# One more seven-product gate pair in chunk 1, batch 4's casts behind the masks, and a sum of u moved in chunk 3

## The chip, the core and the metric

The kernel runs on one core of one Trainium2 chip. The metric is the device time of a whole execution in microseconds (us), as the median of several runs. TensorE (PE) does the matrix products, VectorE (DVE), ScalarE (ACT) and GpSimd (POOL) the elementwise work, and the queues of SyncE (SP), POOL and ACT issue the transfers. Everything is float16 on chip, with float32 sums.

## The reference

Attention over 8 batches and 8 heads (576 positions, 64 wide), then a gated feed-forward block over all 4608 tokens:

```python
mask_plain = (rel >= 0) & (rel < 32)
mask_dil = (rel >= 0) & (rel < 128) & (rel % 4 == 0)
# heads 0..3 take mask_plain, heads 4..7 take mask_dil
attn = softmax(where(mask, q @ k.T / 8, -1e9))
x = (attn @ v).transpose(0, 2, 1, 3).reshape(4608, 512)
g = x @ w_gate                          # 512 -> 1536
val = x @ w_val                         # 512 -> 1536
out = (gelu(g) * val) @ w_out           # 1536 -> 512
```

## The kernel before

The tokens are cut into 9 chunks of 512. A chunk `c` has two stages. In its gate stage the two products with `w_gate` and `w_val` are made for 12 column blocks `nb` of 128, ACT takes the gelu of the one (`g`, L1032), and DVE multiplies it with the other into `u_all` (`u`, L1037). In its output stage `u_all` is multiplied with `w_out`, and between these products stands the attention of later tokens: four pairs of heads `n`, four to a batch, so that pairs 16 to 19 are batch 4. For a pair there are scores `S`, their exponential `P` (ACT, L488), the product with the 0/1 mask `M` (DVE, L493), denominators `D`, numerators `N`, logarithm and reciprocal `l`, `r` (ACT), and the product `X` into `xT` (DVE, L618). In output stage 2 the pairs 12 to 15 are worked on, and at its end stand the scores of pairs 16 and 17.

From chunk 1 on the output product of a pair of blocks uses seven half-size products for eight (`seven`, L816). It needs sums of `u` on DVE (`u_sums`, word `k j@part@n`: part 0 is L777, part 1 L782, part 2 L784; part 2 is read by the last product alone) and sums of `w_out`, made once (`weight_sums`, word `K i@part`, L764 to L770). The gate products of some block pairs `j` (blocks 2j and 2j+1) are done the same way in chunks 2 to 8 (`IN_PLACES`): word `f j@product@bank` is four matmuls of 256 columns (L696), whose results ACT keeps (L710, L718) or DVE adds (`quarter`, L720), with a gelu and a product by halves (L728, L737). That needs four sums of x (`x_sums`, word `x`, L678: DVE in chunks 1 and 2, POOL in chunks 3 to 7) and four sums of the gate weights, once (`gate_sums`, word `h`, L661). Pair 1's are made in output stage 0 already.

The order on every engine is written by hand: `gate_words(c)` and `out_words(c)` give a list of words; a number takes so many matmuls off the chunk's list, and each other word emits the instructions of one step. `BLOCKS[c]` gives, for the directly computed blocks, how many `f` steps follow each half block and which words stand there. Each engine works its own instructions in that order, and waits on semaphores for the others.

A batch comes in by float32 loads into three areas of `stage`, casts on POOL into `s16` (`cast_plain`, L217, two for q and two for k; `cast_dil`, L229), and four DMA transposes from `s16` into the q/k buffer (`turn`, L272): plain q, plain k, dilated q, dilated k, in this order. The load of dilated k goes into the area that plain q was in, and so waits for plain q's casts. All these loads, the transposes, the loads of v and the stores of results are issued by SP in program order, with one queue. Word `R`, at the start of gate stage 2, emits the rest of batch 3 and all of batch 4.

TensorE is kept busy from the start by 69 matmuls of 32x32 and four of 512 columns on a constant (`warm`, L909) before the first data come.

Of the kernel before, what the change touches and what calls it, by code (L numbers as in the profile page):

```python
# [14 lines left out]
SYNC = mybir.DependencyInfo(mybir.DependencyClass.Sync, mybir.DependencyReason.DATA)  # L15
# [6 lines left out]
def kernel(  # L22
# [10 lines left out]
    nc = tc.nc  # L33
    B, H, S, D = q.shape
# [177 lines left out]
            rest = src[b, x * HK : x * HK + HK, S - 64 : S, :].rearrange("h p d -> p h d")  # L212
            nc.sync.dma_start(out=st[64 * x : 64 * x + 64, 4], in_=rest)

    def cast_plain(t, i):
        for g in range(2):
            nc.gpsimd.tensor_copy(  # L217
                s16[:, 1280 * t + 640 * g : 1280 * t + 640 * g + 640].rearrange("p (k c) -> p k c", k=5),
                st_of(i).rearrange("p (k g c) -> p k g c", k=5, g=2)[:, :, g],
            )  # L220

    def load_dil(src, b, i):
        rows_ = src[b, HK:H, 0 : 4 * P, :].rearrange("h (p r) d -> p h (r d)", r=4)
# [48 lines left out]
        nc.sync.dma_start_transpose(out=dst, in_=src)  # L272
# [695 lines left out]
    def gate_banks(c, nb):  # L968

        if c == 0:  # L970
            return ((4, 5), (6, 7))[nb] if nb < 2 else ((0, 1), (2, 3))[nb % 2]
        if c in IN_SEVEN:
            if c == NCH - 1:
                return (3, 5) if nb == 10 else (0, 7)
            if c == NCH - 2:
                return (2, 5) if nb == 10 else (0, 7)
            if nb in (1, 11):
                return (1, 4)
            return (4, 1) if nb == 9 and c < 4 else (0, 7)
        return ((0, 7), (1, 6) if c == 1 else (1, 4))[nb % 2]  # L980

    SEVEN = range(1, NCH)

# [29 lines left out]
    def run_program(c, words, mms, banks):  # L1013

        units = {"S": two_s, "M": two_m, "D": two_den, "N": two_num, "T": two_t, "B": two_b, "X": two_x, "A": two_a, "l": two_l, "r": two_r, "P": two_p_of, "t": turn_first, "y": turn_second, "c": cast_six, "W": idle, "b": bias_first}
        joint = {"S": two_s_mms, "D": two_den_mms, "N": two_num_mms}
        for word in words.split():
            kind, args = word[0], [] if "+" in word else [int(x) for x in word[1:].split("@") if x]
            if "+" in word:
                lists = []  # L1020
                for part in word.split("+"):
                    n, at = (int(x) for x in part[1:].split("@"))
                    lists.append((joint[part[0]](n, at), odd(n)))
                emit_tiles(*lists)
            elif kind.isdigit():
                for _ in range(int(word)):
                    mms.pop(0)()
            elif kind in units:
                units[kind](*args)
            elif kind == "g":  # L1030
                g = ffn.tile([P, CH], F16, tag="g")
                nc.scalar.activation(g, ps[:, gate_banks(c, args[0])[0], :], AF.Gelu)  # L1032
                tiles["g", args[0]] = g
            elif kind == "u":
                nb = args[0]
                val = ps[:, gate_banks(c, nb)[1], :]
                nc.vector.scalar_tensor_tensor(u_all[:, nb, :], tiles.pop(("g", nb)), -USCALE if c in SEVEN and nb % 2 else USCALE, val, ALU.mult, ALU.mult)  # L1037
            elif kind in "ew":
                at = args[1] if len(args) > 1 else c
                store(at, args[0], out_banks(at)[args[0]], "act" if kind == "e" else "dve")  # L1040
            elif kind == "k":
                u_sums(*args)
            elif kind == "K":
                weight_sums(*args)
            elif kind == "f":
                j, product, place = args
                ffn1_seven(c, j, product, place, product in (1, 2, 7))
                quarter_u()
                quarter_gelu()
                quarter_out(c, j, product, place)  # L1050
            elif kind == "U":
                quarter_u()
                quarter_gelu()
            elif kind == "h":
                gate_sums(*args)
            elif kind == "x":
                x_sums(args[0] if args else c)
            elif kind == "q":
                what, eng, at = (args + [c])[:3]
                part_out(at, what, eng, out_banks(at)[what in (1, 3, 5)])  # L1060
            elif kind == "L":
                mms.clear()
                last_chunk(c)
            elif kind == "V":
                (second, second_v)[args[0] if args else 0]()
            elif kind == "v":
                cast_part(c + 2, args[0], tiles["M"])
            elif kind == "z":
                cast_part(c + 1, args[0])
            elif kind == "F":  # L1070
                load_first(args[0])
            elif kind == "H":
                load_rest(args[0])
            elif kind == "R":
                load_rest(3)
                load_first(4)
                load_rest(4)
            elif kind == "E":
                nc.scalar.preload_act_table_set("natural_log_exp_and_others")
            else:  # L1080
                nc.scalar.preload_act_table_set("gelu_and_others")
        assert not mms

    def gate_words(c):
# [13 lines left out]
        if c == min(SEVEN):  # L1098
            for n, nb in enumerate((1, 2, 2, 4, 4, 4, 5, 6, 6, 8, 8, 8)):
                sums[nb] += f" K{n // 4}@{n % 4}"  # L1100
        before = "" if c == NCH - 1 else f"q6@1@{c - 1}"
        last = f" u{NNB - 1} k5@0 k5@1 k5@2" if c > 6 else ""
        first = "7 G 1 g0 2 u0 4 g1 2 u1" if c < NCH - 1 else ""
        if c in IN_SEVEN:
            words = seven_words(c)
            loads = f"{loads} x" if c == 2 else f"x z0 z1 {loads}" if c == 3 else f"x z1 {loads}" if c < 6 else "x z1 h3@0 h3@1 h3@2 h3@3" if c < 7 else "x" if c < NCH - 1 else loads
# [4 lines left out]
        if c == 1:  # L1111
            blocks[8] += f" S{2 * NHP}@12+S{2 * NHP + 1}@14"
        rest = " ".join(blocks)
        if c == 1:
            return f"{loads} 8 G 3 g0 1 u0 3 g1 1 u1{sums[1]} {rest} 4 g{NNB - 1} 4"
        return f"{before} {loads} {first}{sums[1]} {rest} 4 g{NNB - 1} 4{last}"

    one = (
# [46 lines left out]
    def out_words(c):  # L1165

        if c == 0:
            return (
                "h1@0 h1@1 h1@2 h1@3 V1 F2 S6@4+S7@6 1 E P6 11 P7 1 M6 S4@4+S5@6 M7 1 P4 6 P5 M4 2 D6@40+D7@60 l6 l7 M5 r6 r7 6 w2@0 4 w1@0 4 "
                "w0@0 H2 N6@50+N7@20 D4@52+D5@22 X6 l5 X7 l4 r4 r5 10 N4@20+N5@40 X4 X5 2 e3@0"  # L1170
            )
# [4 lines left out]
        some = "k5@1@2 k5@2@2" if len(IN_SEVEN.get(c, ())) < 2 else "k5@1@2@3 k1@2@2 k3@2@2 k5@2@2"  # L1176
# [54 lines left out]
```

## Time and profile before

| | |
|---|---|
| median of 3 runs | 314.6 us (313.5 to 315.01) |
| the profiled execution | 313.68 us, of it 312.0 us span |
| granted TensorE clock | 1.00 of full speed |
| PE, DVE, ACT, POOL busy | 305.8, 233.9, 190.1, 120.4 us |
| gate stages of chunks 1, 2, 3 | from 55.0, 88.1 and 121.4 us |
| output stages of chunks 0, 1, 2, 3 | from 41.1, 76.3, 109.0 and 144.8 us |

The span is the time from the first instruction to the last on the core; some 1.7 us of the execution lie around it. In rows of groups, the name of a tile is followed by what it is made from; "x12" is a count, and the time in brackets at the end of a row of the timeline is the engine's idle time before it, with what ended it. SPq and POOLq are the queues' own instructions.

### The profile page before, as it was taken

How to read it: one execution, taken by the hardware profiler on the slowest of the kernel's cores; microseconds unless marked ns; L12 is line 12 of the kernel's file. 1: busy time of each engine (PE TensorE's matmuls, PEld its weight loads, DVE VectorE, ACT ScalarE, POOL GpSimd, SP SyncE). 2: the span in 40 equal slices, each digit the busy share in tenths (PEclk: the TensorE clock that was granted, in tenths of full speed). 3: DMA queues.
4: the chain of work that ended last, by engine and by line, in shares of the span. 5: the costliest groups of instructions: out<-in, count | busy, mean ns of one | idle time of the engine just before them, and what ended most of it. 6: DMA issues, size and time to landing. Idle time of an engine off the chain costs nothing.

```text
span 312.0 us, 8940 instructions
## 1 busy us (share of the span) xinstructions
PE 305.8 (98%) x3657; PEld 199.9 (64%) x3657; DVE 233.9 (75%) x434; ACT 190.1 (61%) x325; POOL 120.4 (39%) x170
## 2 busy tenths in 40 slices
PE   7999999999999999999999999999999999999995
PEld 4754555445855586557766785668666877687674
DVE  6863665797887895598769985998679858966972
ACT  2573476534774586547767676777577777427640
POOL 8884783312476253534266037513840050000000
PEclk9999999999999999999999999999999999999999
DMA  8999999897799999989799967975200220021004
GB/s 186 193 201 206 204 199 150 249 210 192 162 294 168 195 210 164 244 197 222 165 241 249 168 177 172 229 165 148 69 3 1 69 69 2 0 96 40 2 1 136
DMA packets 110793, 47.18 MB, mean 151 GB/s; under 512 B 83616, under 2 KB 110240, under 8 KB 110752
## 3 DMA queue, kind: packets, MB, share of 16 engines
q1 hardware_dynamic: 97248, 38.29, 55.6%
q0 software_dynamic: 12944, 7.67, 17.4%
q10 hardware_dynamic: 560, 0.66, 0.8%
q8 instruction: 28, 0.46, 0.6%
q14 instruction: 13, 0.11, 0.1%
HBM read 37.75 MB, written 9.44 MB: 151 GB/s over the span
## 4 chain that ended last, share of the span: by engine, by line
PE 90%; DVE 3%; ACT 2%; DMA 2%; issue 1%; POOL 1%; ACTq 0%
PE ps L627 42%; PE ps L816 22%; PE ps L696 14%; PE ps L458 6%; PE ps L741 3%; DMA xT<-in_k_dram 2%; ACT P L488 1%; PE ps L378 1%; DVE u_all L1037 1%; ACT lg L588 1%; DVE ux L777 1%; DVE P L493 0%; PE ps L447 0%; DVE u_all L784 0%; DVE u_all L737 0%
## 5 line engine op out<-in xcount | busy, mean ns | idle before, releaser
L627 PE MATMUL ps<-xT,wv 128*128 128x512 f16 x320 | 83.4, 379 | 0.0
L627 PE MATMUL ps<-xT,wg 128*128 128x512 f16 x320 | 82.6, 379 | 0.0
L1037 DVE SCALAR_TENSOR_TENSOR u_all<-g,ps 128x512 f16<-128x512 f16 x80 | 54.6, 685 | 37.1 <-PE ps L627 17.6
L1032 ACT ACTIVATE g<-ps 128x512 f16<-128x512 f32 x80 | 47.7, 597 | 53.5 <-PE ps L627 53.4
L627 PEld LDWEIGHTS <-wg 128*128 128x128 f16 x320 | 31.0, 98 | 31.9
L627 PEld LDWEIGHTS <-wv 128*128 128x128 f16 x320 | 31.3, 98 | 30.9 <-issue 0.6
L816 PEld LDWEIGHTS <-u_all 128*128 128x128 f16 x390 | 36.3, 98 | 7.0 <-issue 0.3
L816 PE MATMUL ps<-wx,ux 128*128 128x256 f16 x288 | 35.4, 272 | 0.2 <-DVE vdiag L861 0.2
L816 PE MATMUL ps<-wo,u_all 128*128 128x256 f16 (+1 forms) x294 | 35.2, 271 | 0.1
L488 ACT ACTIVATE P<-ps 128x832 f16<-128x832 f32 (+1 forms) x32 | 25.3, 834 | 11.3 <-PE ps L458 11.2
L217 POOL CAST s<-stage 128x640 f16<-128x640 f32 x24 | 18.6, 801 | 34.8 <-DMA stage<-in_q_dram 22.8
L816 PEld LDWEIGHTS <-ux 128*128 128x128 f16 x288 | 28.0, 98 | 4.5 <-issue 0.4
L254 POOL CAST v<-stage 128x1152 f16<-128x1152 f32 x11 | 13.5, 1229 | 39.6 <-DMA stage<-in_v_dram 31.3
L618 DVE TENSOR_TENSOR xT<-ps,rb 128x576 f16<-128x576 f32 x32 | 23.2, 751 | 6.1 <-PE ps L458 4.4
L696 PEld LDWEIGHTS <-xT 128*128 128x128 f16 x224 | 21.9, 98 | 8.9 <-issue 0.3
L777 DVE TENSOR_TENSOR ux<-u_all 128x512 f16<-128x512 f16 x48 | 24.2, 511 | 0.8
L737 DVE SCALAR_TENSOR_TENSOR u_all<-g,quarter 128x256 f16<-128x256 f16 x50 | 22.3, 448 | 3.0 <-ACT g L728 2.9
L728 ACT ACTIVATE g<-quarter 128x256 f16<-128x256 f32 x50 | 20.4, 415 | 6.6 <-DVE quarter L720 6.6
L678 POOL TENSOR_TENSOR x_sum<-xT 128x512 f16<-128x512 f16 x10 | 11.5, 1154 | 32.1 <-DVE xT L618 32.1
L696 PE MATMUL ps<-x_sum,xT 128*128 128x256 f16 x168 | 22.9, 273 | 0.0
L588 ACT ACTIVATE lg<-ps 128x576 f32<-128x576 f32 x30 | 18.6, 655 | 7.1 <-PE ps L458 4.1
L594 ACT ACTIVATE rb<-lg 128x576 f32<-128x576 f32 x30 | 19.0, 688 | 0.1
(120 smaller groups left out, 436.6 us busy)
## 6 DMA issues: line engine op xcount, KB each, us to landing
out_dram<-part SPq DMA_DIRECT2D x30, 256.0 KB, 3.1
stage<-in_v_dram SPq DMA_DIRECT2D x28, 144.0 KB, 3.7
stage<-in_q_dram SPq DMA_DIRECT2D x24, 128.0 KB, 3.5
stage<-in_k_dram SPq DMA_DIRECT2D x24, 128.0 KB, 2.9
stage<-in_q_dram SPq DMA_DIRECT2D x6, 512.0 KB, 4.5
stage<-in_k_dram SPq DMA_DIRECT2D x6, 512.0 KB, 5.3
stage<-in_v_dram SPq DMA_DIRECT2D x20, 128.0 KB, 3.2
wo<-in_moe_w_out_dram POOLq DMA_DIRECT2D x3, 512.0 KB, 15.7
```

Source lines behind the costliest of these rows:

```text
L488: nc.scalar.activation(pt[:, 0 : src.shape[1]], src, AF.Exp, bias=0.0, scale=scale)
L588: nc.scalar.activation(to, den, AF.Ln)
L594: nc.scalar.activation(rb, tiles.pop(("lg", n)), AF.Exp, scale=-1.0)
L618: nc.vector.tensor_tensor(dst, num, rb, ALU.mult)
L627: nc.tensor.matmul(ps[:, bank, :], w[:, kc, ns], xT[kc][:, tok], start=first, stop=end)
L696: nc.tensor.matmul(ps[:, bank, 2 * P * m : 2 * P * m + 2 * P], left[:, k], right[:, k], start=first and m == 0 and k == 0, stop=k == 1, sk ...
L728: nc.scalar.activation(g, t[:, 0 : 2 * P], AF.Gelu)
L737: nc.vector.scalar_tensor_tensor(dst, g, by, t[:, 2 * P : 4 * P], ALU.mult, ALU.mult)
L777: nc.vector.tensor_tensor(ux[:, j, 0:2], k0, u_all[:, 2 * j : 2 * j + 2, hi], ALU.subtract)
L816: lambda o=o, s=s[:, P * p : P * p + P], t=t[:, c0:c1], st=st, end=end: nc.tensor.matmul(o, s, t, start=st, stop=end, skip_group_check=True)
L1032: nc.scalar.activation(g, ps[:, gate_banks(c, args[0])[0], :], AF.Gelu)
L1037: nc.vector.scalar_tensor_tensor(u_all[:, nb, :], tiles.pop(("g", nb)), -USCALE if c in SEVEN and nb % 2 else USCALE, val, ALU.mult, ALU.mult)
```

## The change

Chunk 1's block pair 1 (blocks 2 and 3) is computed with seven products, as in chunks 2 and 3, with banks and order taken from there. Chunk 1's gate words are therefore made by `seven_words`; the four x sums come at its start, on DVE. Of the twelve weight sums six move from gate stage 1 to output stage 0. To keep the number of TensorE instructions, 12 of the first warming matmuls go, and the 57 that stay have 40 columns for 32.

Word `R` of gate stage 2 now emits only the loads of batch 4; the casts, the load of dilated k and what follows are emitted by a new word `C` in output stage 2, behind the masks of pairs 12 and 13, and the casts of plain q and k wait for these masks.

In chunk 3 part 2 of the sums of u for pairs 0 and 1 (`k1@2@2`) moves from the end of the gate stage to behind the masks of pairs 16 and 17 in output stage 3.

```diff
-    def cast_plain(t, i):
+    def cast_plain(t, i, behind=None):
...
+            if behind is not None:
+                tc.add_manual_dep(ins.ins, behind.ins.name, SYNC, reason="masks first")
...
     def load_first(b):
+        load_raw(b)
+        cast_first(b)
+
+    def load_raw(b):
         load_plain(q, b, 0)
         load_plain(k, b, 1)
         load_dil(q, b, 2)
-        cast_plain(0, 0)
-        cast_plain(1, 1)
+
+    def cast_first(b, behind=None):
+        cast_plain(0, 0, behind)
+        cast_plain(1, 1, behind)
         load_dil(k, b, 0)
...
+    IN_PLACES[1] = {1: (1, 4)}
...
-    warm(69, 7, 32, 32)
+    warm(57, 7, 32, 40)
...
             elif kind == "R":
                 load_rest(3)
-                load_first(4)
+                load_raw(4)
+            elif kind == "C":
+                cast_first(4, tiles["M"])
                 load_rest(4)
...
-    BLOCKS[3] = (*one, "", "")
+    BLOCKS[3] = (one[0], one[1].replace("k1@2@2", ""), "", "")
+    BLOCKS[1] = (
+        one[0],
+        one[1].replace("||k0@0||k2@0||||k3@0|", "K1@2|K1@3|k0@0 K2@0|K2@1|k2@0|K2@2||K2@3|k3@0|").replace("k1@2@2", "k1@2@2 S8@12+S9@15"),
...
-        v0 = " v0" if 2 < c < 6 else ""
-        some = "k5@1@2 k5@2@2" if len(IN_SEVEN.get(c, ())) < 2 else ...
+        v0 = " v0" if 2 < c < 6 else " C" if c == 2 else ""
+        some = "k5@1@2 k1@2@2 k5@2@2" if c == 3 else ...
```

On POOL the order of the instructions stays as it was. The rows show the end of batch 3's work in gate stage 2 (a v load, the copy into the dilated q of batch 3) and the first casts of batch 4. Before:

```order
L332 DMA v_100<-in_v_dram 64x9x64 [waits DMASW7_49]
L332 DMA v_100<-in_v_dram 64x9x64 [waits DMASW0_49]
L297 COPY q_105<-q_105 128x8x16 [waits DVE_49,DMAHW6_49,PE_49,Activation_49]
L217 CAST s_107<-stage 128x640 [waits DMAHW5_49,DMAHW4_49,DMAHW6_49,DMAHW3_49,DMAHW7_49,DMAHW2_49,Pool_49]
L217 CAST s_107<-stage 128x640 [waits Pool_49]
L217 CAST s_107<-stage 128x640 [waits DMAHW3_49,DMAHW2_49,DMAHW4_49,DMAHW1_49,DMAHW5_49,DMAHW0_49,Pool_49]
```

The same place on POOL in the change:

```order
L340 DMA v_100<-in_v_dram 64x9x64 [waits DMASW7_49]
L340 DMA v_100<-in_v_dram 64x9x64 [waits DMASW0_49]
L305 COPY q_105<-q_105 128x8x16 [waits DVE_49,DMAHW6_49,PE_49,Activation_49]
L217 CAST s_107<-stage 128x640 [waits DMAHW4_49,DMAHW5_49,DMAHW3_49,DMAHW6_49,DMAHW2_49,DMAHW7_49,DVE_49,Pool_49]
L217 CAST s_107<-stage 128x640 [waits Pool_49]
L217 CAST s_107<-stage 128x640 [waits DMAHW3_49,DMAHW2_49,DMAHW4_49,DMAHW1_49,DMAHW5_49,DMAHW0_49,Pool_49]
```

Nothing has moved; the first cast has one more wait, for DVE (the masks), and what is behind it on POOL stays behind it.

On DVE the end of gate stage 3 and the start of output stage 3 stand as follows before (L1037 makes `u` of blocks 10 and 11, L861 copies the first product, P16 and P17 are masked):

```order
L782 TENSOR_TENSOR ux_109<-u_all_108,ux_109 128x2x256
L1037 SCALAR_TENSOR_TENSOR u_all_108<-g_2509,ps_114 128x512
L784 TENSOR_TENSOR u_all_108<-ux_109,u_all_108 128x2x256
L1037 SCALAR_TENSOR_TENSOR u_all_108<-g_2523,ps_114 128x512
L777 TENSOR_TENSOR ux_109<-u_all_108 128x512
L861 TENSOR_SCALAR vdiag_103<-ps_114 128x512
L493 TENSOR_TENSOR P16_2530<-P16_2530,two_p_81 128x832
L493 TENSOR_TENSOR P17_2532<-P17_2532,two_p_81 128x832
```

The same place on DVE in the change:

```order
L791 TENSOR_TENSOR ux_109<-u_all_108,ux_109 128x2x256
L1046 SCALAR_TENSOR_TENSOR u_all_108<-g_2534,ps_114 128x512
L1046 SCALAR_TENSOR_TENSOR u_all_108<-g_2547,ps_114 128x512
L786 TENSOR_TENSOR ux_109<-u_all_108 128x512
L870 TENSOR_SCALAR vdiag_103<-ps_114 128x512
L501 TENSOR_TENSOR P16_2554<-P16_2554,two_p_81 128x832
L501 TENSOR_TENSOR P17_2556<-P17_2556,two_p_81 128x832
L791 TENSOR_TENSOR ux_109<-u_all_108,ux_109 128x2x256
L793 TENSOR_TENSOR u_all_108<-ux_109,u_all_108 128x2x256 x2
```

The sum of u (L784 before, L793 now) is gone from between the two products of `u` and stands behind the masks, where there are now two of it in a row.

On DVE, between output stage 0 and the start of gate stage 1, the change has (wx0 to wx2 are the weight sums, x_sum the sums of x, L763 a store's copy; the rows of L626 are `X`):

```order
L763 TENSOR_SCALAR osb_1046<-ps_114 128x512
L626 TENSOR_TENSOR xT_99<-ps_114,rb_1022 128x576
L626 TENSOR_TENSOR xT_99<-ps_114,rb_1024 128x576
L626 TENSOR_TENSOR xT_99<-ps_114,rb_1132 128x576
L626 TENSOR_TENSOR xT_99<-ps_114,rb_1134 128x576
L687 TENSOR_TENSOR x_sum_1194<-xT_99 128x512
L687 TENSOR_TENSOR x_sum_1193<-xT_99,x_sum_1194 128x512
L687 TENSOR_TENSOR x_sum_1195<-xT_99 128x512
L687 TENSOR_TENSOR x_sum_1196<-xT_99,x_sum_1193 128x512
L1046 SCALAR_TENSOR_TENSOR u_all_108<-g_1235,ps_114 128x512
L1046 SCALAR_TENSOR_TENSOR u_all_108<-g_1242,ps_114 128x512
L777 TENSOR_TENSOR wx1_111<-wo1_97 128x512
```

Before, the first product of `u` followed on the last `X` there:

```order
L754 TENSOR_SCALAR osb_1052<-ps_114 128x512
L618 TENSOR_TENSOR xT_99<-ps_114,rb_1028 128x576
L618 TENSOR_TENSOR xT_99<-ps_114,rb_1030 128x576
L618 TENSOR_TENSOR xT_99<-ps_114,rb_1138 128x576
L618 TENSOR_TENSOR xT_99<-ps_114,rb_1140 128x576
L1037 SCALAR_TENSOR_TENSOR u_all_108<-g_1233,ps_114 128x512
L1037 SCALAR_TENSOR_TENSOR u_all_108<-g_1240,ps_114 128x512
L777 TENSOR_TENSOR ux_109<-u_all_108 128x512
L764 TENSOR_TENSOR wx0_110<-wo0_96 128x512
```

The four sums of x have come in between, and weight sums wx0 are no longer made in the gate stage.

More of the change, by code (lines that the diff above doesn't have):

```diff
@@ L213, in load_plain @@
             nc.sync.dma_start(out=st[64 * x : 64 * x + 64, 4], in_=rest)
-    def cast_plain(t, i):
+    def cast_plain(t, i, behind=None):
         for g in range(2):
-            nc.gpsimd.tensor_copy(
+            ins = nc.gpsimd.tensor_copy(
                 s16[:, 1280 * t + 640 * g : 1280 * t + 640 * g + 640].rearrange("p (k c) -> p k c", k=5),
@@ L977, in gate_banks @@
             if nb in (1, 11):
-                return (1, 4)
+                return (1, 6 if c + nb == 2 else 4)
             return (4, 1) if nb == 9 and c < 4 else (0, 7)
-        return ((0, 7), (1, 6) if c == 1 else (1, 4))[nb % 2]
+        return ((0, 7), (1, 4))[nb % 2]
     SEVEN = range(1, NCH)
@@ L1097, in gate_words @@
                 sums[2 * j + 1] += f" k{j}@0" + (f" k{j}@1@2 k{j}@2@2" if j % 2 else "")
[L1098 to L1101, printed above, removed]
+        before = "" if c in (1, NCH - 1) else f"q6@1@{c - 1}"
         last = f" u{NNB - 1} k5@0 k5@1 k5@2" if c > 6 else ""
         first = "7 G 1 g0 2 u0 4 g1 2 u1" if c < NCH - 1 else ""
+        if c == 1:
+            first, loads = "8 G 3 g0 1 u0 3 g1 1 u1", f"x {loads}"
         if c in IN_SEVEN:
             words = seven_words(c)
-            loads = f"{loads} x" if c == 2 else f"x z0 z1 {loads}" if c == 3 else f"x z1 {loads}" if c < 6 else "x z1 h3@0 h3@1 h3@2 h3@3" if c < 7 else "x" if c < NCH - 1 else loads
+            loads = loads if c == 1 else f"{loads} x" if c == 2 else f"x z0 z1 {loads}" if c == 3 else f"x z1 {loads}" if c < 6 else "x z1 h3@0 h3@1 h3@2 h3@3" if c < 7 else "x" if c < NCH - 1 else loads
             if c == NCH - 2:
@@ L1110, in gate_words @@
         blocks = [f"4 g{nb} 4 u{nb}{sums[nb]}" for nb in range(2, NNB - 1)]
-        if c == 1:
-            blocks[8] += f" S{2 * NHP}@12+S{2 * NHP + 1}@14"
         rest = " ".join(blocks)
-        if c == 1:
-            return f"{loads} 8 G 3 g0 1 u0 3 g1 1 u1{sums[1]} {rest} 4 g{NNB - 1} 4"
         return f"{before} {loads} {first}{sums[1]} {rest} 4 g{NNB - 1} 4{last}"
@@ L1126 @@
     BLOCKS = {c: (*two, "", "") for c in range(4, 7)}
-    BLOCKS[3] = (*one, "", "")
+    BLOCKS[3] = (one[0], one[1].replace("k1@2@2", ""), "", "")
+    BLOCKS[1] = (
+        one[0],
+        one[1].replace("||k0@0||k2@0||||k3@0|", "K1@2|K1@3|k0@0 K2@0|K2@1|k2@0|K2@2||K2@3|k3@0|").replace("k1@2@2", "k1@2@2 S8@12+S9@15"),
+        "",
+        "",
+    )
     early = "h2@0||k0@0 h2@1||k2@0||h2@2||k3@0 h2@3|"
@@ L1174, in out_words @@
         i, j, k, l = (NHP * (c + 1) + n for n in range(NHP))
-        v0 = " v0" if 2 < c < 6 else ""
-        some = "k5@1@2 k5@2@2" if len(IN_SEVEN.get(c, ())) < 2 else "k5@1@2@3 k1@2@2 k3@2@2 k5@2@2"
+        v0 = " v0" if 2 < c < 6 else " C" if c == 2 else ""
+        some = "k5@1@2 k1@2@2 k5@2@2" if c == 3 else "k5@1@2 k5@2@2" if len(IN_SEVEN.get(c, ())) < 2 else "k5@1@2@3 k1@2@2 k3@2@2 k5@2@2"
         after = f"S{l + 1}@12+S{l + 2}@15" if 1 < c < 6 else ""
```

2 lines of the change are left out of this document (1 added, 1 removed).

## The prediction

> **What bounds the kernel now.** I read the page's busy times first, then PE's own waits, then each engine's busy time in the stages that the change touches (a row gives the stretch, its length, busy time and count of PE, PEld, DVE, ACT and POOL, the granted clock, the mean number of busy DMA shares and GB/s).
>
> ```profile
> PE 305.8 (98%) x3657; PEld 199.9 (64%) x3657; DVE 233.9 (75%) x434; ACT 190.1 (61%) x325; POOL 120.4 (39%) x170
> ```
> ```profile
> PE ps L816 <- DVE vdiag L861: 0.2, 1, 0.2
> ```
> ```profile
> 41.10:55.00 13.90, 13.89 (x245) 6.99 (x246) 7.81 (x11) 9.04 (x13) 7.72 (x11) 1.00 1.07 170
> 55.00:76.30 21.30, 21.30 (x135) 9.78 (x133) 17.33 (x34) 9.25 (x15) 5.65 (x8) 1.00 0.93 214
> 88.10:109.00 20.90, 20.90 (x147) 10.92 (x145) 17.57 (x39) 11.30 (x21) 11.23 (x17) 1.00 1.41 213
> 121.40:144.80 23.40, 23.17 (x134) 12.77 (x132) 17.13 (x30) 14.20 (x24) 12.76 (x15) 1.00 0.88 222
> ```
>
> PE works 305.8 of 312.0 us, and in the gate stages of chunks 1 and 2 it is busy from end to end. So only two things count: columns taken off PE, and the few places where PE does or would wait. Of those there is one in these stages: chunk 3 lacks 0.23 us, and the copy L861 ends the wait. DVE has 4 us of air in chunk 1.
>
> **Part 1, the pair in chunk 1.** The chain shows the same two kinds of product side by side in chunk 2 (start, length, count):
>
> ```profile
> 99.36 0.44 PE ps L696 x4
> 99.79 0.86 PE ps L627 x4
> ```
>
> Pair 1 has two blocks of two products, each four matmuls of 512 columns: 4 x 0.86 = 3.44 us. Seven products of four matmuls of 256 columns are 7 x 0.44 = 3.08. That is -0.36 by these rows; by counted columns (16 x 512 against 28 x 256, at 0.86 for 2048) it is 3.44 against 3.01, -0.43. I take **-0.4**. PE pays nothing else, if the operands are in time. DVE pays (groups, with the mean in ns behind the comma):
>
> ```profile
> L678 DVE TENSOR_TENSOR x_sum<-xT 128x512 f16<-128x512 f16 x4 | 2.1, 522 | 0.0
> L678 DVE TENSOR_TENSOR x_sum<-xT,x_sum 128x512 f16<-128x512 f16 x4 | 2.4, 596 | 0.1
> L720 DVE TENSOR_TENSOR quarter<-ps,vdiag 128x512 f32<-128x512 f32 x20 | 13.7, 685 | 4.5 <-PE ps L696 3.8 <-ACT vdiag L710 0.6
> L737 DVE SCALAR_TENSOR_TENSOR u_all<-g,quarter 128x256 f16<-128x256 f16 x50 | 22.3, 448 | 3.0 <-ACT g L728 2.9
> L1037 DVE SCALAR_TENSOR_TENSOR u_all<-g,ps 128x512 f16<-128x512 f16 x80 | 54.6, 685 | 37.1 <-PE ps L627 17.6 <-ACT g L1032 15.5 <-ACT turned L710 2.6
> L764 DVE TENSOR_TENSOR wx<-wo 128x512 f16<-128x512 f16 x3 | 1.2, 416 | 0.0
> L766 DVE TENSOR_TENSOR wx<-wx,wo 128x512 f16<-128x512 f16 x3 | 1.3, 442 | 0.0
> L768 DVE TENSOR_TENSOR wx<-wo 128x512 f16<-128x512 f16 x3 | 1.7, 552 | 0.0
> L770 DVE SCALAR_TENSOR_TENSOR wx<-wx,wo 128x512 f16<-128x512 f16 x3 | 2.0, 683 | 0.0
> ```
>
> Added to the stage: four sums of x (2 x 0.522 + 2 x 0.596 = 2.24), three quarters (2.06) and four half products (1.79). Taken out: two whole products (1.37), and the six weight sums that leave for output stage 0 (parts 2 and 3 of one block row, 0 to 3 of the next: 0.42 + 0.44 + 0.55 + 0.68 + 0.42 + 0.44 = 2.95). Net +1.77, so DVE goes from 17.33 of 21.3 to 19.1 of 20.9. That is fuller than chunk 2 (17.57 of 20.9), where PE lost nothing. Where do the sums of x fit? Ahead of the first `u`:
>
> ```profile
> 58.05 0.69 DVE L1037 SCALAR_TENSOR_TENSOR u_all<-g,ps 128x512 f16<-128x512 f16 x1 [2.04 <-ACT g L1032]
> ```
>
> DVE idles 2.04 us there, and the sums take 2.24: the first product is 0.2 late at most, which the rest of DVE's air takes up. The weight sums find 13.9 - 7.81 = 6.1 free in output stage 0 and are not read before output stage 1. ACT goes from 9.25 of 21.3 to less than chunk 2's 11.3 of 20.9. I cost all this at nothing; if the cover is gone, the price is what DVE has more, up to 1.77 (rival D).
>
> **Part 2, the warming matmuls.**
>
> ```profile
> L909 PE MATMUL ps<-ones 128*32 128x32 f16 x69 | 2.0, 188 | 1.5 <-DVE ones L67 1.5
> 6.08 0.28 PEld L375 LDWEIGHTS <-s 96*128 96x128 f16 x6 [0.36 <-DVE s L360]
> ```
>
> 69 of 32 columns take 2.0 in all, 0.029 each; 57 of 40 columns take, if columns set it, 57 x 0.036 = 2.07, if the count does, 1.65. Either way the first real work waits on DVE's cast with 0.36 in hand: 0.
>
> **Part 3, batch 4's casts behind the masks.** The casts of plain q and plain k on POOL, the masks on DVE with these casts beside them, and masks of the same shape with no cast beside them:
>
> ```profile
> 107.61 1.58 POOL L217 CAST s<-stage 128x640 f16<-128x640 f32 x2 [8.74 <-DMA stage<-in_q_dram]
> 110.47 1.71 POOL L217 CAST s<-stage 128x640 f16<-128x640 f32 x2 [1.28 <-DMA stage<-in_k_dram]
> 110.97 1.62 DVE L493 TENSOR_TENSOR P<-P,two_d 128x768 f16<-128x768 f16 x2
> 148.27 1.02 DVE L493 TENSOR_TENSOR P<-P,two_d 128x768 f16<-128x768 f16 x2
> 109.21 0.37 SPq L224 DMA_DIRECT2D stage<-in_k_dram  x1
> ```
>
> The masks of pairs 12 and 13 begin at 110.97 and will end between 112.0 (1.02, alone) and 112.6; I take 112.2. So the first cast starts 4.6 later. Plain q's casts end at 112.2 + 1.58 = 113.8, where before they ended at 109.19, and SP could issue the load of dilated k at 109.21. SP works in order: this load, the four transposes, the loads of v, the stores of stage 2 and batch 5's loads all start about 4.6 later, less what slack takes up. Before, the turn of plain k was issued when its casts ended (110.47 + 1.71 = 112.18); the issue takes 2.24 us, and the row below it gives the time to landing:
>
> ```profile
> L272 SPq DMA_TRANSPOSE q<-s x1: 2241/2241/2241, 112.2 to 112.2; - x1
> DMA to landing us min/median/max: 5.6/5.6/5.6
> ```
> ```profile
> L272 SPq DMA_TRANSPOSE q<-s x1: 2212/2212/2212, 140.9 to 140.9; - x1
> DMA to landing us min/median/max: 4.1/4.1/4.1
> ```
> ```profile
> 120.11 0.54 PE L458 MATMUL ps<-q 64*64 64x96 f16 x36
> 152.96 0.54 PE L458 MATMUL ps<-q 64*64 64x96 f16 x36
> ```
>
> So batch 4's plain k landed at 117.8, 2.3 ahead of the scores of pairs 16 and 17, which read it on PE at 120.11. With the change SP issues the load at 113.8, the turn of plain q at about 114.1, and the turn of plain k 2.2 later, at 116.3 (plain k's casts are done at 113.8 + 1.7 = 115.5, so SP sets it). The same turn in batch 5 took 4.1 to land: 120.4, 0.3 late. With the 5.6 of before it lands at 121.9, 1.8 late; with the full 4.6 of shift at 122.4, 2.3 late. Nothing stands behind the scores on PE that may pass them, so lateness is a stall one for one. Which of these is near? The 5.6 held a pause, and a pause comes again:
>
> ```profile
> 115.00:116.00 1.00, 1.00 (x11) 0.82 (x10) 1.00 (x3) 1.00 (x3) 0.36 (x1) 1.00 0.13 6
> 119.00:120.00 1.00, 1.00 (x35) 0.74 (x37) 0.84 (x2) 1.00 (x2) 0.00 (x0) 1.00 2.09 77
> ```
> ```profile
> q8 instruction: 1, 0.02, 7.4%
> ```
>
> From 115 to 116 all queues together moved 6 GB/s, from 119 to 120 only 77, and the last row, of the microsecond before the first of these, shows a block fetched for an engine's instructions. The pause at 119 falls at a place in PE's program that does not move (the change keeps the number of PE's instructions), so the later turn meets it where the earlier one met that at 115. I take +1.3, between 0.3 and 2.3, nearer to the 5.6 than to the 4.1. The Trainium skill (Runtime: NRT & Kernel Launch, section Instruction fetch mechanics) says that an engine's sequencer fetches its program in blocks of 16 KiB by a queue of its own, and that crossing a boundary is mostly hidden; by that the turn would take 4.1, the stall be 0.3, and the sum -0.55. For the engines' own work the trace agrees, for the other queues the 6 GB/s speaks against it.
>
> Batch 5's plain k turn comes later too, from 140.9 + 4.1 = 145.0 to at most 149.6, before its scores at 152.96: 0.
>
> **Part 4, the sum moved in chunk 3.**
>
> ```profile
> 142.88 1.67 PE L816 MATMUL ps<-wx,ux 128*128 128x256 f16 x12
> 144.76 0.49 PE L816 MATMUL ps<-wx,ux 128*128 128x256 f16 x3 [0.20 <-DVE vdiag L861]
> 142.01 0.79 DVE L784 TENSOR_TENSOR u_all<-ux,u_all 128x512 f16<-128x512 f16 x1
> 142.71 0.67 DVE L1037 SCALAR_TENSOR_TENSOR u_all<-g,ps 128x512 f16<-128x512 f16 x1
> 143.42 0.68 DVE L777 TENSOR_TENSOR ux<-u_all 128x512 f16<-128x512 f16 x1
> 144.03 0.68 DVE L861 TENSOR_SCALAR vdiag<-ps 128x512 f32<-128x512 f32 x1
> ```
>
> Twelve matmuls of 256 columns at 0.109 are 1.31, so PE was through at 144.19; the next began at 144.76. Those 0.57 us hang on DVE's row of last product, sum and copy, with the moved sum (0.79) at its head. Without it the row is up to 0.7 earlier and the stall gone. It is read by the last product alone, and behind the masks it still comes in time. The gain lies between 0 (another link sets the end) and 0.57; I take **-0.45**, since the row is DVE's own from end to end.
>
> **Sum.** -0.4 + 0 + 1.3 - 0.45 = **+0.45**. The profiled execution took 313.68 us (312.0 of span and 1.7 around), 0.9 below the median of 314.6: 314.1 for such an execution, **315.0** for the median.
>
> **Rivals.** A is the forecast: plain k 0.8 to 1.9 late, together -0.1 to +1.1, 314.5 to 315.7.
>
> B, the rows come in time or 0.3 late. For it: the 4.1 of batch 5, and that the turn starts after the pause at 115. Then -0.4 - 0.45 + 0.15 = -0.7: 313.9; at best, with 0.57 won, 313.6. The page's rule on fetches gives this one.
>
> C, the other side: the shift of 4.6 comes through whole, plain k lands at 122.4 or later, and the stall is 2.3. The later casts of batch 5 then also run into the masks of pairs 16 and 17 (1.62 for 1.02, 0.6 more on DVE) and the chunk 3 gain is gone. -0.4 + 2.3 = +1.9: 316.5. It decides from a stall of 2.0, a landing after 122.1. Against it: SP would have to be held up twice, at the load and at the turn.
>
> D, the pair doesn't pay: at 19.1 of 20.9 DVE sets the pace in chunk 1, half of its 1.77 more is paid by PE, and with the other terms it is -0.4 + 0.9 + 1.3 - 0.45 = +1.35: 315.9. Against it are chunk 2 with the same order and the whole 21.3 without a gap before.
>
> **How the numbers follow.** A 0.50, B 0.27, C 0.15, D 0.08. About 0.5% (1.57 us) is what a measurement of this kernel can tell from no change. Slower than 316.2 are most of C, a third of D and little of A: 0.15. Faster than 313.0 would need B's best and 0.6 of luck: 0.06. Same 0.79. The range goes from B's best with 0.2 of spread in the runs, 313.4, to just over C, 316.6.
>
> **What would show it.** Chunk 1: 28 more L696 rows of 256 columns in its gate stage, which is 20.9 long with PE full; a PE gap there means D. The first batch 4 cast begins at 111.6 to 112.2 (all before it comes 0.4 earlier). Plain k's turn is issued near 116 and lands after 120, with a PE wait on that transpose ahead of S16 as the largest of PE's waits; none means B, over 2.0 means C. PE's wait on L861 is gone. I am wrong beyond these if the late load or stores push batch 5's rows past 152.96, which is nowhere in my sum.

## The result, and the profile after

The changed kernel takes 316.24 us (median of 22 runs, 314.41 to 317.54), the kernel before, beside it, 314.06 (22 runs): 1.0066 times as long, 95% interval [1.0052, 1.008], or 2.1 us slower (2.2 between the two medians). The runs of the changed kernel fall into two groups: in 11 of them the mean granted clock reads 0.998 to 1.00 (median 315.63), in the other 11 it reads 0.992 to 0.995 (median 317.06). The kernel before shows 0.998 to 1.00 in all of the runs that stood beside the experiments. The profiled execution of the changed kernel is one of the first group: 315.41 us, span 313.7.

The page's chain of work that ended last, by engine, before and after:

```profile
PE 90%; DVE 3%; ACT 2%; DMA 2%; issue 1%; POOL 1%; ACTq 0%
```
```profile
PE 73%; DMA 10%; SPq 8%; POOL 3%; ACT 2%; DVE 2%; issue 1%; POOLq 0%
```

Before, the chain ran on PE almost throughout. Now 18% of the span are SP's queue and transfers: somewhere PE waits for a load path that reaches far back. PE's own waits, after, name the place (total, times, longest):

```profile
PE ps L466 <- DMA q<-s: 1.9, 1, 1.9
...
PE ps L466 <- issue: 0.5, 1, 0.5
```

The first is the scores of pairs 16 and 17 waiting for a turn. The wait on the copy L861 at the end of chunk 3 is gone from the list. Batch 4's path after, from the timeline (POOL, then SP's queue, then the masks) and, as the last three rows, from the chain of the same stretch:

```profile
112.48 2.98 POOL L217 CAST s<-stage 128x640 f16<-128x640 f32 x4 [13.18 <-DMA stage<-in_q_dram]
```
```profile
114.16 0.37 SPq L226 DMA_DIRECT2D stage<-in_k_dram  x1
114.63 7.55 SPq L274 DMA_TRANSPOSE q<-s  x4
```
```profile
111.13 1.23 DVE L501 TENSOR_TENSOR P<-P,two_d 128x768 f16<-128x768 f16 x2
```
```profile
116.10 5.95 DMA q<-s
122.05 0.04 issue
122.09 0.56 PE ps L466 x36
```

The masks end at 112.36, the first cast starts at 112.48 (107.61 before), the load of dilated k is issued at 114.16 (109.21 before), the turn of plain k at 116.10 (112.2 before). It takes 5.95 us, and PE starts the scores when it has landed.

Where the time went, stage by stage, from the first product of a stage to the first of the next in the two traces:

| | before | after | |
|---|---|---|---|
| start of gate stage 1 | 54.85 | 55.25 | +0.40 |
| gate stage 1 | 21.29 | 20.89 | -0.40 |
| output stage 1 | 11.81 | 11.98 | +0.17 |
| gate stage 2 | 20.90 | 20.90 | 0 |
| output stage 2 | 12.40 | 14.24 | +1.84 |
| gate stage 3 | 20.32 | 20.32 | 0 |
| output stage 3 | 12.75 | 12.29 | -0.46 |
| from there to the last matmul | 153.98 | 154.12 | +0.14 |
| last matmul starts | 308.30 | 309.99 | +1.69 |

By these starts output stage 3 begins at 141.57 before; the 144.8 of the table ahead of the prediction is where PE goes on after the copy L861. In these two traces the pair and the moved sum bring what was forecast in their own stages, -0.40 and -0.46; output stage 2 gives back more than twice that. The 0.17 of output stage 1 comes from the masks of the first two pairs there (DVE, before and after, then POOL's cast of v beside them):

```profile
78.26 1.61 DVE L493 TENSOR_TENSOR P<-P,two_d 128x768 f16<-128x768 f16 x2
78.26 1.96 DVE L501 TENSOR_TENSOR P<-P,two_d 128x768 f16<-128x768 f16 x2
```
```profile
77.85 1.15 POOL L254 CAST v<-stage 128x1152 f16<-128x1152 f32 x1 [2.54 <-DMA stage<-in_v_dram]
78.36 1.45 POOL L256 CAST v<-stage 128x1152 f16<-128x1152 f32 x1 [2.73 <-DMA stage<-in_v_dram]
```

The masks start at the same time and take 0.35 longer, with more of the cast beside them, and PE's denominators wait for them. The stage is 11.97 to 12.16 long in seven of the nine traces that have the pair (11.80 and 11.81 in the others) and 11.81 in all four without it, so this is not of one execution; that the pair makes the two overlap was not tested. The 0.40 at the start is PE's idle time of 0.5 with "issue" in the list above, near 13.7 us; the run of the warming matmuls alone, below, takes that one up.

### The profile page after: what moved, and what is told of

The parts are those of the page before. It is cut to its first block, busy times and chain, and to the rows that moved or that the text cites. A ratio compares the mean times of both kernels' runs of the same rounds, so it can differ in the third digit from the quotient of the medians.

```text
span 313.7 us, 8956 instructions
## 1 busy us (share of the span) xinstructions
PE 305.2 (97%) x3657; PEld 201.2 (64%) x3657; DVE 238.3 (76%) x443; ACT 192.4 (61%) x331; POOL 120.9 (39%) x170
## 4 chain that ended last, share of the span: by engine, by line
PE 73%; DMA 10%; SPq 8%; POOL 3%; ACT 2%; DVE 2%; issue 1%; POOLq 0%
PE ps L635 33%; PE ps L825 17%; PE ps L705 13%; PE ps L466 5%; DMA q<-s 4%; PE ps L750 3%; SPq L210 3%; DMA stage<-in_q_dram 3%; SPq L274 2%; DMA xT<-in_q_dram 2%; SPq L213 1%; DMA stage<-in_v_dram 1%; POOL s L231 1%; PE ps L386 1%; ACT P L496 1%
## 5 line engine op out<-in xcount | busy, mean ns | idle before, releaser
L635 PE MATMUL ps<-xT,wv 128*128 128x512 f16 x312 | 81.4, 379 | 0.0
L1046 DVE SCALAR_TENSOR_TENSOR u_all<-g,ps 128x512 f16<-128x512 f16 x78 | 53.3, 686 | 36.4 <-PE ps L635 17.3
L635 PE MATMUL ps<-xT,wg 128*128 128x512 f16 x312 | 80.6, 380 | 0.0
L1041 ACT ACTIVATE g<-ps 128x512 f16<-128x512 f32 x78 | 46.5, 597 | 50.1 <-PE ps L635 49.9
L635 PEld LDWEIGHTS <-wg 128*128 128x128 f16 x312 | 30.2, 98 | 30.3
L705 PEld LDWEIGHTS <-xT 128*128 128x128 f16 x240 | 23.5, 98 | 10.0 <-issue 0.3
L626 DVE TENSOR_TENSOR xT<-ps,rb 128x576 f16<-128x576 f32 x32 | 23.2, 752 | 8.4 <-PE ps L466 3.7
L746 DVE SCALAR_TENSOR_TENSOR u_all<-g,quarter 128x256 f16<-128x256 f16 x54 | 24.4, 455 | 3.0 <-ACT g L737 2.9
L737 ACT ACTIVATE g<-quarter 128x256 f16<-128x256 f32 x54 | 22.1, 414 | 6.8 <-DVE quarter L729 6.6
L705 PE MATMUL ps<-x_sum,xT 128*128 128x256 f16 x180 | 24.7, 273 | 0.0
L596 ACT ACTIVATE lg<-ps 128x576 f32<-128x576 f32 x30 | 18.7, 655 | 6.9 <-PE ps L466 3.9
L231 POOL CAST s<-stage 128x512 f16<-128x512 f32 x24 | 16.8, 726 | 8.1 <-DMA stage<-in_q_dram 6.2
```

Source lines behind the costliest of these rows:

```text
L231: nc.gpsimd.tensor_copy(s16[:, at : at + 512].rearrange("p (r h d) -> p h r d", r=4, h=2), st_of(i)[:, 512 * g : 512 * g + 512].rearrange( ...
L596: nc.scalar.activation(to, den, AF.Ln)
L626: nc.vector.tensor_tensor(dst, num, rb, ALU.mult)
L635: nc.tensor.matmul(ps[:, bank, :], w[:, kc, ns], xT[kc][:, tok], start=first, stop=end)
L705: nc.tensor.matmul(ps[:, bank, 2 * P * m : 2 * P * m + 2 * P], left[:, k], right[:, k], start=first and m == 0 and k == 0, stop=k == 1, sk ...
L737: nc.scalar.activation(g, t[:, 0 : 2 * P], AF.Gelu)
```

## The experiments

Theory 1 was that the late rows alone make the loss, and the low clock follows from PE's idle time; its rivals were the pair (2), the warming matmuls (3), and a pause that belongs to the turns (4). Every ratio is against runs of the kernel before in the same set.

**The wait alone, on the kernel before.**

```diff
-                load_first(4)
+                load_raw(4)
+            elif kind == "C":
+                cast_first(4, tiles["M"])
                 load_rest(4)
...
-        v0 = " v0" if 2 < c < 6 else ""
+        v0 = " v0" if 2 < c < 6 else " C" if c == 2 else ""
```

> The kernel before with part 3 alone (batch 4's casts behind the masks of pairs 12 and 13). Theory 1, the late rows: the changed kernel's one large wait, 2.0 us ahead of the scores of pairs 16 and 17, comes from the wait of the casts alone. Then this kernel has it too, and is 2.0 us slower than before (some 316.1 against 314.1); in the runs where the mean granted clock reads 0.993 it is a further 1.5 slower. Rival 2, the extra comes from the pair: this kernel is at most 1.3 slower and its clock reads 1.00 or 0.998 in every run. Rival 3, the warming matmuls: no low clock here, and no idle PE at 13 us.

Measured: 317.32 (6 runs), ratio 1.0103 [1.007, 1.0136], 3.2 us slower; three of six runs read 0.993 to 0.995. Two of the other three, at 1.0, took 317.2 and 317.3, so the low clock is not all of the spread. The wait is the whole loss, more than the changed kernel's, whose other parts pay some of it back. The profiled execution has the low clock, and its windows show how it comes (stretch, length, busy time and count of PE, PEld, DVE, ACT, POOL, granted clock, DMA share, GB/s):

```profile
118.68:122.09 3.41, 1.58 (x83) 1.23 (x80) 0.91 (x2) 1.53 (x3) 0.79 (x2) 1.00 1.30 167
122.09:125.50 3.41, 3.41 (x28) 1.64 (x16) 1.42 (x2) 1.77 (x2) 1.69 (x2) 0.50 0.76 193
125.50:128.91 3.41, 3.41 (x18) 1.57 (x17) 1.27 (x2) 1.30 (x3) 3.39 (x4) 1.00 0.39 95
```
```profile
121.69 0.59 PE L466 MATMUL ps<-q 64*64 64x96 f16 x36 [1.83 <-DMA q<-s]
122.21 1.46 PE L824 MATMUL ps<-wo,u_all 128*128 128x256 f16 x6
```

The trace records one stretch of exactly 3.413 us at half clock, right behind the stretch of the same length in which PE idled for want of the turn: busy 1.58 of 3.41. PE works all through the slow stretch and does half the work, so it loses another 1.7 us (six matmuls of 256 columns took 1.46 there; without the wait, in the next experiment, they take 0.83). The Trainium skill (TensorE: Matmul & The Clock Gate, section What's actually happening) says that the clock is set from activity in free-running windows of 3.413 us; the trace has that length to the nanosecond. The same page of the Trainium skill (section Why this matters for your kernels) asks only for no idle gaps of over about 3 us; here 1.8 in one window was enough.

**The changed kernel without the wait.**

```diff
-                load_raw(4)
+                load_first(4)
+                load_rest(4)
...
-        v0 = " v0" if 2 < c < 6 else " C" if c == 2 else ""
+        v0 = " v0" if 2 < c < 6 else ""
```

> The changed kernel with batch 4's casts back at the start of gate stage 2 (pair in chunk 1, warming matmuls and moved sum stay). Theory 1: no wait at 120 us; -0.4 of the pair and -0.57 of chunk 3's end remain, +0.5 if PE's idle time at 13.7 us is there again: 0.4 to 1.0 us faster than before, 313.1 to 313.7, with no run at a clock of 0.993. Rival 2: the runs split into two groups 1.5 us apart here as well, the slower at 0.993, and the median is above before's.

Measured: 313.5 (12 runs), ratio 0.9977 [0.9956, 0.9998], 0.7 faster; the clock is 0.998 or more in all runs. PE's timeline at the same scores has no idle time and the matmuls behind them at full clock:

```profile
120.03 0.54 PE L466 MATMUL ps<-q 64*64 64x96 f16 x36
120.50 0.83 PE L825 MATMUL ps<-wo,u_all 128*128 128x256 f16 x6
```

So neither the pair nor the moved sum costs anything that these runs show, or lowers the clock. This version is the fastest so far, against the kernel before by little (the interval ends at 0.9998). SP, POOL, DVE and ACT work the same instructions in the same order in this trace and in the changed kernel's, so the wait is all that differs there.

**The pair alone** (this kernel with chunk 3's sum back in its place) **and the sum alone** (the kernel before with it moved). The edit shown is that of the second; the first is the version without the wait with this edit taken back.

```diff
-    BLOCKS[3] = (*one, "", "")
+    BLOCKS[3] = (one[0], one[1].replace("k1@2@2", ""), "", "")
...
-        some = "k5@1@2 k5@2@2" if len(IN_SEVEN.get(c, ())) < 2 else ...
+        some = "k5@1@2 k1@2@2 k5@2@2" if c == 3 else ...
```

> The kernel before with part 1 and part 2 (pair in chunk 1, 57 warming matmuls) and nothing else. The prediction's step: 0.4 faster than before, some 313.8 against 314.2, with no gap on PE in gate stage 1. If VectorE became the bound there (rival D), it is 0.5 or more slower.

> The kernel before with part 4 alone (the sum moved in chunk 3). The prediction's step: PE's wait on the copy L861 at the end of chunk 3 (0.57 us between matmuls) is gone, and the time 0.45 below before. If another link sets the end there, it equals before.

Measured: pair 313.91, ratio 0.9995 [0.9975, 1.0016]; sum 313.85, ratio 0.9988 [0.9972, 1.0004]. Both point the right way and neither is clear of no change: 12 runs don't resolve 0.4 us. Their traces do better: gate stage 1 is 21.03 long with the pair for 21.29 (20.89 to 21.04 in seven other traces that have it, 21.27 in that of the turns first, below), and the wait on the copy L861 of chunk 3 is gone with the sum moved. Gate stage 1 and the same place in chunk 3, both in the changed kernel:

```profile
55.25:76.14 20.89, 20.89 (x146) 10.91 (x144) 18.68 (x37) 11.14 (x21) 5.64 (x8) 1.00 0.91 213
```
```profile
144.89 2.35 PE L825 MATMUL ps<-wx,ux 128*128 128x256 f16 x20
```

In the first PE is full and DVE busy for 18.68 of 20.89; rival D does not show here. It does for once in the trace of the turns first, where PE waits 0.21 at 64.78 for DVE's product of `u`. In the second, 20 matmuls follow on one another where 12 and 8 had a gap between them. What the stages keep is less sure than the place itself: with output stage 1 the pair's two stages are 32.84 to 33.20 long in the nine traces that have it, for 33.10 before, and output stage 3 is 12.53 long with the sum alone, only 0.22 less than before.

**The warming matmuls alone.**

```diff
-    warm(69, 7, 32, 32)
+    warm(57, 7, 32, 40)
```

> The kernel before with 57 warming matmuls of 40 columns for 69 of 32. Rival 3, 12 fewer instructions move the places where PE's program is fetched: PE idles about 0.5 us near 13.7 us with no semaphore named, and the time is 0.3 to 0.5 above before. If the idle time at 13.7 in the changed kernel was of that one execution, this kernel is within 0.2 of before.

Measured: 313.94, ratio 0.999 [0.997, 1.0009]. No cost in the median, though its profiled execution idles 1.4 near 13.5 us, with no semaphore named:

```profile
PE ps L458 <- issue: 1.5, 2, 1.4
```

The same idle time is 0.5 and 0.3 in the traces of the changed kernel and of the pair alone, and absent in those of the five other kernels with 57 of them. With the old 69 and no wait it should vanish:

> The changed kernel without the wait of the casts (as in the run that took it away alone), and with the old warming matmuls, 69 of 32 columns. If the 57 cost something (three of seven traces with them show PE idle 0.5 to 1.5 us near 13.5 us with no semaphore named, none of three with 69): 0.3 faster than with 57, 0.9 to 1.0 below before. Else equal to the run without the wait, 0.7 below before.

Measured: 313.6, ratio 0.9982 [0.9962, 1.0002], as without (0.9977). It comes and goes between traces of kernels that start alike, and the median doesn't show it; most of the +0.40 of the table is luck of that execution.

**More and less of the wait.** The first cast waits for the sums of `u` behind the masks (L793, kept as `U`; below, with word `C` behind these sums), or for the mask of pair 12 alone (`M0` in the same place).

```diff
-                cast_first(4, tiles["M"])
+                cast_first(4, tiles["U"])
...
-        v0 = " v0" if 2 < c < 6 else " C" if c == 2 else ""
+        v0 = " v0" if 2 < c < 6 else ""
...
+        if c == 2:
+            some += " C"
```

> The changed kernel with the first cast waiting for the sums of u behind the masks, about 1.2 us later. Theory 1a (the wait is paid one for one, and where enough of it falls into one 3.41 us window of the clock's gate, the next window runs at half clock): the wait ahead of the scores of pairs 16 and 17 is about 3.2, so that some window holds at least 1.6 of it in every run: nearly all runs are at a clock of 0.995 or less, and the median is 316.2 + 1.2 + 0.8 = some 318. Rival: the low clock has to do with something else than this wait (the denser PE stage before it, the run's phase): then the share of runs at 0.993 stays about half, and the median is some 317.4.

> The changed kernel with the first cast waiting for the mask of pair 12 alone, about 0.6 us earlier. Theory 1a: the wait at the scores is about 1.4, less than half of a window of 3.41, and no run has a low clock; the time is 0.6 below the fast group of the changed kernel (315.5), some 314.9, and the runs don't split. Rival as above: half the runs still at 0.993, median some 315.6.

Measured: longer 317.31 (6 runs), ratio 1.0097 [1.0069, 1.0125], five of six runs at 0.993 to 0.995; shorter 315.19 (12 runs), ratio 1.002 [1.0003, 1.0038], none below 0.998. PE's waits, longer and shorter:

```profile
PE ps L466 <- DMA q<-s: 2.2, 1, 2.2
```
```profile
PE ps L466 <- DMA q<-s: 1.4, 1, 1.4
```

I expected 3.2 for the longer: its casts came only 0.6 later (113.07), so the price was 317.3 for 318. The sign holds: of these three kernels none of the runs with a wait of 1.4 has the low clock, half of those with 1.9, and nearly all with 2.2. The windows on the gate's grid (starts worked out from the trace's change of clock in steps of 3.413 us) show the bound, first the longer, then the shorter, then the changed kernel:

```profile
119.73:123.14 3.41, 1.16 (x72) 0.96 (x61) 0.40 (x1) 0.60 (x2) 0.40 (x2) 1.00 0.91 166
123.14:126.55 3.41, 3.41 (x12) 1.38 (x10) 1.02 (x2) 1.88 (x2) 2.16 (x2) 0.50 0.75 186
```
```profile
119.33:122.74 3.41, 2.05 (x85) 1.61 (x84) 1.15 (x3) 0.89 (x3) 0.00 (x0) 1.00 1.45 169
122.74:126.15 3.41, 3.41 (x17) 1.57 (x16) 1.21 (x2) 2.87 (x4) 2.65 (x3) 1.00 0.57 162
```
```profile
118.05:121.46 3.41, 2.17 (x56) 1.71 (x53) 1.89 (x3) 2.14 (x4) 1.47 (x3) 1.00 1.29 161
121.46:124.87 3.41, 2.78 (x50) 1.82 (x51) 1.42 (x2) 1.40 (x2) 0.73 (x1) 1.00 0.95 215
```

PE busy 1.16 or 1.58 of a window: the next one is at half clock. Busy 2.05 or more: it is not. Two other traces lie in between, that of the scores later (next section) and the end of the one without the wait:

```profile
159.47:162.88 3.41, 1.83 (x12) 0.97 (x10) 1.54 (x3) 0.87 (x3) 3.33 (x3) 1.00 1.03 324
162.88:166.29 3.41, 3.20 (x22) 2.10 (x22) 2.07 (x3) 2.24 (x5) 2.55 (x3) 1.00 0.77 174
```
```profile
307.03:310.44 3.41, 1.69 (x19) 1.39 (x16) 0.66 (x3) 0.77 (x2) 0.00 (x0) 1.00 0.77 254
310.44:312.20 1.76, 0.00 (x0) 0.00 (x0) 0.00 (x0) 0.00 (x0) 0.00 (x0) 1.00 0.00 0
```

After 1.83 and 1.69 the clock stays at 1.00. So the bound lies between 1.58 and 1.69 of 3.41, a little under half. In the changed kernel's profiled execution the wait straddles a border of the grid, 1.2 on one side and 0.6 on the other, so the clock held. Where the grid lies differently, the same wait should cost 1.4 more (317.06 against 315.63); no trace of such a run of the changed kernel was kept, and the two traces with the low clock stand for it. An estimate from these numbers fits: by the bound a window must hold 1.72 to 1.83 us of idle time (3.41 less 1.69 or 1.58), a wait of 1.87 puts that much into one window in 48 to 54% of its possible places on the grid, and 11 of 22 runs read low.

**The scores later.** Nothing on PE reads batch 4's rows before gate stage 3.

```diff
-    BLOCKS[3] = (one[0], one[1].replace("k1@2@2", ""), "", "")
+    BLOCKS[3] = (one[0], one[1].replace("k1@2@2", "").replace("U k1@0", "U k1@0 S16@12+S17@15"), "", "")
...
-        after = f"S{l + 1}@12+S{l + 2}@15" if 1 < c < 6 else ""
+        after = f"S{l + 1}@12+S{l + 2}@15" if 2 < c < 6 else ""
```

> The changed kernel with the scores of pairs 16 and 17 moved from the end of output stage 2 into gate stage 3, so that nothing on PE reads batch 4's rows before about 130 us; the casts still wait for the masks. Theory 1: the rows are as late as in the changed kernel but nobody waits, so 0.4 to 1.0 us faster than before (313.1 to 313.7). If the late transfers cost something elsewhere (stores, batch 5), it stays at before or above.

Measured: 315.76 (12 runs), ratio 1.0044 [1.0018, 1.0071]; two of twelve runs read 0.993 and 0.995. The wait at 120 is gone, and another stands 40 us later, in gate stage 4 (PE's wait list, and POOL's timeline):

```profile
PE ps L705 <- POOL x_sum L687: 1.8, 2, 1.3
```
```profile
158.27 1.15 POOL L256 CAST v<-stage 128x1152 f16<-128x1152 f32 x1 [9.07 <-DMA stage<-in_v_dram]
159.38 1.32 POOL L687 TENSOR_TENSOR x_sum<-xT 128x512 f16<-128x512 f16 x1
```

Without the wait of the casts this cast of v starts at 154.83. The sums of x stand behind that cast on POOL and come late for PE. SP's late queue is a part of it: SP issues the last loads of v from 154.65 here, from 151.53 without the wait. But in the changed kernel, with the same shift at 120, they are issued from 153.25 and the cast starts at 156.04; the second sum is ready at 159.53, and PE reads it at 161.92. So by these times some 0.5 us would be left there even without PE's own wait of 1.9. Why batch 5's turns and loads are later still in this run I have not traced.

**The instruction fetch moved.**

```diff
-    warm(57, 7, 32, 40)
+    warm(13, 7, 32, 175)
```

> The changed kernel with 13 warming matmuls of 175 columns for 57 of 40: the same columns, 44 matmuls and their 44 weight loads fewer, so that each block of PE's program is fetched 88 instructions later in the work. Theory 1b (the block fetched while the turns are under way halts all queues, and this pause is what makes the turn take 5.9 us for 4.1): the fetch of 119.1 falls behind 120, where PE already waits, and the one of 112.8 at some 113.9, just ahead of the late transfers. The pause then stands ahead of them (0.0 to 0.7 of delay) and not among them: plain k lands at 120.8 to 121.5 instead of 122.05, the wait is 0.8 to 1.5, no run at 0.993, median some 315. Rival 4, the pause belongs to the turns themselves (the third follows the second at its own time): the pause stays at 119.8 to 121, the wait stays 2.0 and the time 316.2.

Measured: 314.82 (11 runs), ratio 1.0023 [0.9997, 1.005], 1.4 below the changed kernel. One run of 11 reads 0.994, which a wait of 0.9 doesn't explain; no trace of it was kept. In the changed kernel a block of PE's program (16 KB, the queue of instructions) is fetched at 119.14, here at 120.34. All queues of the core together, first the changed kernel, then this one:

```profile
119.80:121.10 1.30, 0.42 (x40) 0.31 (x32) 0.14 (x1) 0.77 (x2) 0.14 (x1) 1.00 0.12 6
121.10:122.10 1.00, 0.01 (x2) 0.01 (x3) 0.00 (x0) 0.00 (x0) 0.00 (x0) 1.00 1.25 281
```
```profile
119.80:121.10 1.30, 0.75 (x39) 0.67 (x40) 0.27 (x1) 0.02 (x1) 0.00 (x0) 1.00 2.17 181
121.10:122.00 0.90, 0.90 (x9) 0.62 (x7) 0.90 (x2) 0.29 (x1) 0.00 (x0) 1.00 0.14 8
```
```profile
PE ps L466 <- DMA q<-s: 0.9, 1, 0.9
```

The pause (1.3 us at 6 GB/s, here 0.9 at 8) has moved with the fetch, to behind the landing. The turn is issued 0.8 later (116.86), lands in 3.45 us for 5.95, and the wait fell from 1.9 to 0.9. Rival 4 falls. The packets of the trace before show the same at all seven fetches that met turns under way (64.5, 98.2, 114.4, 118.8, 146.6, 173.4, 202.1): 0.6 to 1.0 us after the fetch begins, all queues stop for 0.9 to 1.3 us; at 80.3 and 123.3, with no turn under way, none.

**The turns ahead of the load of dilated k.**

```diff
-                cast_first(4, tiles["M"])
-                load_rest(4)
+                cast_plain(0, 0, tiles["M"])
+                cast_plain(1, 1, tiles["M"])
+                load_rest(4, True)
...
         turn(kp.rearrange("p g (k c) -> p (g k) c", c=P), s16[:, 1280:2560])
+        if turns_first:
+            load_dil(k, b, 0)
+            cast_dil(0, 2)
+            cast_dil(1, 0)
         turn(qd.rearrange("p g r i -> p (g r) i")[:, :, 0:P], s16[:, 2560:3584])
```

> The changed kernel with SP's two turns of plain q and k issued ahead of the load of dilated k (512 KB) for behind it. Theory 1c, the load standing ahead in SP's queue is part of the lateness: the plain k turn is issued at 115.5 to 116 (its casts set it) and has no load ahead of it, so it lands some 1 to 1.5 us earlier; the wait is 0.5 to 1.0, the clock 1.00 in all runs, some 315. If the pause sets the landing whatever is ahead, it stays at 2.0 and 316.2.

Measured: 319.05 (5 runs), ratio 1.0143 [1.0102, 1.0184]. The step asked about did what theory 1c says (the turn of plain k issued at 115.48, the wait 0.7), and the kernel is the slowest of all: the load of dilated k is issued at 117.0 for 114.2, its casts end 3.8 later (123.3 for 119.5), and the sums of x in gate stage 4 wait again:

```profile
PE ps L709 <- POOL x_sum L691: 2.3, 2, 1.8
...
PE ps L470 <- DMA q<-s: 0.7, 1, 0.7
```

Two runs of five read 0.989 and 0.994. Its profiled execution is 1.6 below its median; what the slower ones add I have no trace of.

## Why the prediction was right or wrong

The range (313.4 to 316.6) holds 316.24, and a loss was the forecast's direction; but the number was 315.0, and 0.79 stood on no change that can be told. That the range holds is in part luck: its base was the 314.6 of three runs, and the 22 runs beside the result gave 314.06. As changes, the forecast was +0.45 in a range of -1.2 to +2.0, and the measured +2.1 lies at or just beyond its upper end. Step by step:

- **The pair, -0.4:** right in its stage (-0.40), with DVE at 18.7 for 19.1 and PE full. Output stage 1, where 0.17 goes back to the masks, was not in the sum.
- **The warming matmuls, 0:** right in the median.
- **The casts' shift:** right in each of its times. First cast 112.48 (forecast 112.2), load of dilated k 114.16 (113.8), turn of plain k issued 116.10 (116.3). SP's shift at the turn was 3.9, since slack took up the rest.
- **The landing:** this is the term that failed. I had 120.4 by the turn of batch 5, 121.9 by that of batch 4, and the right mechanism between them: a pause of the queues behind a fetch on PE, at a place in the program that stays. The run with the fetch moved shows it. But having said that the later turn meets the pause whole, I took 1.3, a value between a landing with it and one without. The pause is met or it isn't; with it, the row gave 1.8, and the trace has 1.9 (output stage 2 is 1.84 longer). The term was 0.5 too small.
- **The clock:** not in the sum. I priced PE's lateness "one for one". With a wait of 1.4 no run has the low clock; at 1.9 half the runs have it and are another 1.4 longer, which puts some 0.6 on the median (316.24 against 315.63). No row of before has PE idle for so long between matmuls, so nothing there showed it.
- **The moved sum, -0.45:** right (-0.46 in the stage; the gap of 0.57 at the copy is gone). The run of the sum alone kept 0.22 of it in its trace.
- **Batch 5 at no cost:** right for the changed kernel. The place to watch was not its scores but its v rows and the sums of x behind them, which made PE wait in two of the runs above and were not in the forecast.

With the three measured stages (-0.40, +1.84, -0.46) the sum is +0.98, and the clock's 0.6 makes it 1.6. The measured 2.1 holds some 0.5 more. Output stage 1 gives 0.17 of it; the 0.14 behind output stage 3 is of one execution, and the rest stays open. Rival C had the right time, 316.5, by a wait of 2.3 and a lost gain in chunk 3; neither happened. The wait was 1.9, the gain stayed, and the clock made up the difference.

## What to carry to other kernels

A wait put on an engine's first step is paid by the last in-order queue behind it: here a cast moved by 4.9 us moved SP's loads, turns and v rows, and with each cure at one reader (scores later, turns first) another one waited. Where a cost comes whole or not at all, such as a pause that a transfer meets, take one case or the other for the forecast and leave the middle to the range. In these runs a PE wait of more than about half of 3.41 us cost more than its length, and by luck of the grid: where a kernel's runs split into two groups with two mean clocks, look for such a wait.

## What the runs showed of the hardware that was not expected

- PE's clock went to 0.50 for one window of 3.413 us after a window with PE busy 1.16 or 1.58 us, and stayed at 1.00 after 1.69, 1.83, 2.05 and 2.17.
- While transposing transfers were under way, the fetch of a 16 KB block of PE's program was followed by 0.9 to 1.3 us in which all the core's queues together moved 6 to 8 GB/s in the two stretches shown. The Trainium skill (Runtime: NRT & Kernel Launch, section Instruction fetch mechanics) calls the cost of such a crossing mostly hidden; for PE's own issue that held at 119 us, for the transfers beside it not.
- PE idled 0.3 to 1.4 us near 13.5 us with no semaphore named in three of the nine traces with 57 or fewer warming matmuls, and in none of those with 69.
